# Eight chunks of x, six output stages and a new order list in a fused attention and S5 kernel

## The chip, the cores and the metric

The kernel runs on one core of a Trainium2 chip. The metric is device time in microseconds, the median of several runs. One further execution was taken with the hardware profiler; all rows below come from it.

## What is computed

Two layers over 2048 tokens of width 448, their outputs side by side (896 columns, bf16). Part A is sliding, dilated attention with 16 heads of 28: each token attends to itself and to the tokens 2, 4, ... 14 before it. Part B is a diagonal complex state-space layer (S5).

```python
# A: W, dil = 8, 2
qkv = (x @ wqkv).reshape(B, S, 3, H, Dh)           # q, k, v
idx = pos[:, None] - arange(W) * dil                # 8 keys per query, masked where idx < 0
o = softmax(q . k[idx] * Dh ** -0.5) . v[idx]
a = o.reshape(B, S, D) @ wo
# B: Lam = Lambda_re + i Lambda_im, Lam_bar = exp(dt * Lam)
Bu = x @ B_bar.T
for t in range(L):
    h = Lam_bar * h + Bu[:, t]
y = 2.0 * (h @ Cmat.T).real + x * Dskip
out = concatenate([a, y], -1)
```

## The kernel before

Since the window steps by two, even and odd tokens never meet in part A. The kernel views x as 1024 rows that hold an even and an odd token side by side (896 columns), and keeps it transposed in xA, columns on partitions in seven chunks of 128 (chunk 3 holds the last 64 columns of the even token and the first 64 of the odd one). An odd token so begins in the middle of a chunk, and the tile Wt of the weights holds a second copy for it, shifted by 64 partitions, in chunks 3 to 6; the steps s1v, s2v, s1k, s2k, s1q, s2q make it.

The program is a set of named steps, each with an engine and, where it writes to a double PSUM bank, the number of that bank (U0 to U3). ORDER, a list in the source, says in which order they are written out; so it fixes the order on each engine and on each DMA queue, and the framework adds the waits. A token such as w2f.P0 is the step w2f on TensorE (P) into bank 0; V is VectorE, A ScalarE, G GpSimd, S SyncE, which issues transfers. The steps named in the text:

- xt, xe: 128 rows of x are transposed on TensorE and copied to xA (rows 0 to 511); xa: the remaining rows are transposed by transfers on SyncE.
- v, k, q with a row block 0 to 7: the projections, two times six full matmuls (f, or e and o for the even and odd token) and two of 64 rows (t); ve, ke, qe copy the result out; kt and qt transpose k and q by a transfer.
- b, be, ri, sc, ro, with k and a half 0 or 1: the state-space input, its copy, the rotation, the scan and the rotation back into h. lam, c1, c2 mix the weights of part B (c1 and c2 read CT); g, ge and gp make Gm.
- s, x, a, n with a block and a parity: scores, exp, the products with v, and the normalisation into a tile O. ot transposes O into OT by a transfer on SyncE. Block 8 is the border between blocks; oc0, oc1, oc2 copy its columns from OTb into OT for the blocks 1 to 3, 4 and 5, 6 and 7, and so need ot8 and the ot of these blocks.
- wol loads the output weights wo, in four transfers, into the place of CT. w with a block: OT times wo, as f and t; y with a block: h times C and Gm times x, two parities; it starts from xd, which puts x times Dskip (from the tile xo, loaded by xol) into the odd bank. we and ye cast a bank into an output stage of the tile ys; wo0 to wo7 and yo send a stage to HBM on SyncE. The last y block is split into ya7, yb0, yb1.

A bank is written again when its last reader is done. The score tile s is a single one: a step s waits for the x before it. The list before, from the load of xo on:

```
xol.G a41.P1 ge1.A0 s51.P ri11.V g0.P0 x51.A n4.V1 s80.P ge0.A0 c26.V ot4.S a50.P1 sc110.V x80.A a51.P1 wol.S g2.P0 n5.V1 gp2.A0
s60.P ge2.V0 x60.A a80.P1 ot5.S xd1.V0 n8.V1 y1.P0 sc111.V ot8.S xd0.V1 ro11.V s61.P y0.P1 x61.A ri21.V ye1.A0 yo1.S oc0.A a60.P0
sc210.V ye0.A1 yo0.S a61.P0 s70.P n6.V0 w3t.P1 x70.A w3f.P1 sc211.V ot6.S w0f.P0 we3.A1 wo3.S ro21.V w0t.P0 oc1.A s71.P we0.A0 wo0.S
...
```

The tile ys has ten stages of [2, 448] and lies in the place of Wt; five buffers of rows serve the transposes of q and three those of k; two scratch tiles serve the weight mixes.

Of the kernel before, what the change touches and what calls it, by code (L numbers as in the profile page):

```python
# [37 lines left out]
s11.P tc23.G n0.V1 k5t.P0 x11.A k5f.P0 wtx2.S c24.V a10.P1 ri00.V tc21.G qt3.S ke5.A0 s20.P a11.P1 x20.A q7t.P0 xb1.S
q7f.P0 n1.V1 s21.P qe7.A0 c23.V k6f.P1 x21.A c21.V tc22.G k6t.P1 sc000.V a20.P0 qt4.S ke6.A1 s30.P sc001.V a21.P0
tc20.A kt6.S b20.P1 c22.V x30.A n2.V0 tc25.G kt4.S ro00.V kt5.S s31.P be20.A1 b11.P0 x31.A ot0.S c25.V ri20.V qt5.S  # L40
b31.P1 be11.A0 qt6.S c20.V sc200.V s40.P be31.A1 vg1.S b01.P0 tc12.A tc16.V qt7.S x40.A c16.V c12.V tc15.G ot1.S
sc201.V tc10.A s41.P be01.A0 c10.V a30.P1 a31.P1 c15.V tc14.A b21.P0 vg2.S n3.V1 x41.A tc11.G c14.V ot3.S kb.G c11.V
tc13.A s50.P ot2.S be21.A0 c13.V tc26.G a40.P1 ro20.V x50.A g1.P0 xol.G a41.P1 ge1.A0 s51.P ri11.V g0.P0 x51.A n4.V1
s80.P ge0.A0 c26.V ot4.S a50.P1 sc110.V x80.A a51.P1 wol.S g2.P0 n5.V1 gp2.A0 s60.P ge2.V0 x60.A a80.P1 ot5.S xd1.V0
n8.V1 y1.P0 sc111.V ot8.S xd0.V1 ro11.V s61.P y0.P1 x61.A ri21.V ye1.A0 yo1.S oc0.A a60.P0 sc210.V ye0.A1 yo0.S a61.P0
s70.P n6.V0 w3t.P1 x70.A w3f.P1 sc211.V ot6.S w0f.P0 we3.A1 wo3.S ro21.V w0t.P0 oc1.A s71.P we0.A0 wo0.S w4f.P1 x71.A
ri31.V w5f.P0 w5t.P0 w4t.P1 sc310.V w1t.P2 we4.A1 wo4.S w2t.P3 w1f.P2 we5.A0 wo5.S xd3.V1 w2f.P3 ro31.V we1.A2 wo1.S
# [106 lines left out]
def kernel(  # L154
# [80 lines left out]
    def xbar_x(dst, src, p, n):  # L235
        SP.dma_start_transpose(dst[:, :, n * p:n * p + n], src[n * p:n * p + n, :])
# [12 lines left out]
    SP.dma_start(Wt[0:64, 3, KQ], A_wqkv[384:448, KQ])  # L249

# [82 lines left out]
    def evac(e, o, i):  # L333
        if e == "A":
            ACT.copy(o, i)  # L335
        elif e == "G":
            G.tensor_copy(o, i)
        else:
            V.tensor_copy(o, i)  # L339
# [10 lines left out]

    def paired(name, ps, x, c, w):

        def sums(e, u_, js, tail):
            for j in js:
                seen = begun.setdefault((name, j), set())
                first = not seen
                seen.add(tail)
                if tail:
                    r = slice(64 * j, 64 * j + 64)
                    PE.matmul(ps(u_)[j], x()[r, 3, c], w()[r, 3], start=first, stop=not first, skip_group_check=True)  # L360
                for k in range(0 if tail else 3):
                    PE.matmul(ps(u_)[j], x()[:, 4 * j + k, c], w()[:, 4 * j + k], start=(k == 0 and first), stop=(k == 2 and not first), skip_group_check=True)  # L362
# [121 lines left out]

    for n, cols in (("v", VC), ("k", KC), ("q", QC)):
        def f(e, u_, cols=cols):
            evac(e, Wt[0:64, 4:7, cols], Wt[64:128, 0:3, cols])
# [4 lines left out]
        step["s2" + n] = f
    for b_, (n, i, lo, hi) in enumerate((("0a", 0, 0, 3), ("0b", 0, 3, 7), ("1", 1, 0, 7), ("2", 2, 0, 7), ("3", 3, 0, 7))):
        def xt(b_=b_, w=hi - lo):
            return held_by("x")[b_ % 3][:, 0, :].bitcast(BF16)[:, 0:128 * w].rearrange("p (k t) -> p k t", k=w)

        def f(e, u_, xt=xt, i=i, lo=lo, hi=hi):
            for k in range(lo, hi):
                PE.transpose(xt()[:, k - lo, :], xn[:, i, 128 * k:128 * k + 128], eye[:])
# [20 lines left out]
    def _(e, u_):  # L520
# [58 lines left out]
    for b in range(8):  # L579
        paired(f"v{b}", two, lambda: xA, slice(128 * b, 128 * b + 128), lambda: Wt[:, :, VC])  # L580
# [397 lines left out]
```

## Time and profile before

| | |
|---|---|
| median of 3 runs | 133.15 us |
| lowest, highest | 132.99, 133.58 us |
| the profiled execution's own time | 133.44 us |
| its span, first to last instruction | 131.6 us |
| busy: PE, PEld, DVE, ACT, POOL | 123.5, 63.2, 107.3, 86.6, 47.8 us |
| DMA | 20.83 MB, 158 GB/s on average |

PE is TensorE (PEld its weight loads, which overlap it), DVE VectorE, ACT ScalarE, POOL GpSimd, SP SyncE; SPq is SyncE's transfer queue. L362 is line 362 of the kernel. In a timeline a row gives start, length, engine, line, operation, tile written and tiles read, shape, and in brackets the idle time ahead of it with what ended it. A matmul's length includes its way through the array, so that consecutive ones overlap: what a group costs is read from the start of the next group.

### The profile page before, as it was taken

To read this page: it belongs to the slowest core of one execution; us is meant where nothing else is said; L and a number is where in the kernel's file an instruction comes from. 1 tells how busy PE (TensorE), PEld (TensorE's weight loads), DVE (VectorE), ACT (ScalarE), POOL (GpSimd) and SP (SyncE) were. 2 spreads that over 40 slices of the span, in tenths; PEclk is the share of its full clock that TensorE was granted. 3 is DMA by queue.
4 is the path that set the end of the run, shared out by engine and by line. 5 is a ranking of instruction groups with operands and counts; after the bars stand their busy time and mean duration, and the time that the engine had idled before them with its cause. 6 is when DMAs were issued, how large, how long until landed. Compare 5 with 4: busy or idle time off the path is not lost.

```text
span 131.6 us, 3129 instructions
## 1 busy us (share of the span) xinstructions
PE 123.5 (94%) x1221; PEld 63.2 (48%) x1226; DVE 107.3 (81%) x225; ACT 86.6 (66%) x91; POOL 47.8 (36%) x75
## 2 busy tenths in 40 slices
PE   7899999999999999999999998799999999999960
PEld 2554444443444466544454656545644654445540
DVE  2569999998898999999999999999999999860000
ACT  3249779887999879968698957608797523222230
POOL 7998911899700946660077840000000000000000
PEclk9999999999999999999999999999999999999998
DMA  4999969799899995898979949890452652422222
GB/s 106 371 318 211 230 118 183 124 271 165 174 103 186 216 158 86 175 188 200 199 142 156 221 97 256 198 189 9 140 144 70 229 124 70 139 70 72 70 82 70
DMA packets 54546, 20.83 MB, mean 158 GB/s; under 512 B 46782, under 2 KB 54160, under 8 KB 54528
## 3 DMA queue, kind: packets, MB, share of 16 engines
q1 hardware_dynamic: 53376, 18.70, 69.4%
q0 software_dynamic: 656, 1.50, 4.0%
q10 hardware_dynamic: 496, 0.40, 0.9%
q8 instruction: 11, 0.18, 0.6%
q14 instruction: 7, 0.06, 0.2%
HBM read 5.30 MB, written 3.86 MB: 70 GB/s over the span
## 4 chain that ended last, share of the span: by engine, by line
PE 57%; DVE 29%; issue 4%; DMA 3%; POOL 2%; ACT 1%; SPq 0%; DVEq 0%
PE U L362 14%; PE U L851 11%; PE early L362 8%; PE late L851 4%; DVE rs L755 4%; PE U L854 3%; PE U L727 3%; DVE O L692 3%; PE U L360 3%; DVE natW L540 3%; DMA Wt<-in_A_wqkv_dram 3%; DVE C L540 3%; POOL wtmp L534 2%; DVE ra L742 2%; DVE rb L743 2%
## 5 line engine op out<-in xcount | busy, mean ns | idle before, releaser
L671 ACT ACTIVATE P<-s 128x1920 bf16<-128x1920 f32 (+1 forms) x16 | 28.6, 1786 | 5.7 <-PE s L649 5.6
L727 PE MATMUL U<-xB,WT 128*128 128x512 bf16 x93 | 22.1, 379 | 0.3
L362 PE MATMUL U<-Wt,xA 128*128 128x448 bf16 x90 | 19.7, 353 | 1.0 <-DVE Wt L339 0.5
L362 PEld LDWEIGHTS <-xA 128*128 128x128 bf16 x144 | 12.9, 98 | 15.1 <-issue 4.2
L534 POOL TENSOR_SCALAR wtmp<-CT,p_pah 128x448 f32<-128x448 bf16 x6 | 13.7, 2279 | 12.4 <-DVE rv L745 6.8
L335 ACT CAST ys<-U 128x896 bf16<-128x896 f32 (+1 forms) x11 | 9.5, 871 | 12.0 <-PE U L851 9.2
L851 PEld LDWEIGHTS <-h 128*128 128x128 bf16 x105 | 10.0, 98 | 9.2 <-DVE U L841 0.2
L727 PEld LDWEIGHTS <-WT 128*128 128x128 bf16 x98 | 9.2, 97 | 10.6
L362 PE MATMUL early<-Wt,xA 128*128 128x448 bf16 x54 | 11.7, 354 | 0.0
L335 ACT CAST u<-U 128x1024 bf16<-128x1024 f32 (+1 forms) x8 | 7.2, 905 | 4.5 <-PE U L727 4.4
L692 DVE TENSOR_TENSOR O<-U,rcs 128x896 bf16<-128x896 f32 (+1 forms) x9 | 9.8, 1090 | 0.3
L851 PE MATMUL U<-natW,h 128*128 128x448 bf16 x42 | 9.0, 353 | 0.1
L755 DVE TENSOR_TENSOR_SCAN rs<-p_r,ini,rv 128x512 bf16<-128x512 f32 x7 | 8.8, 1274 | 0.0
L680 PE MATMUL U<-Vt,P 128*128 128x29 bf16 x256 | 8.2, 176 | 0.6 <-DVE O L692 0.6
L755 DVE TENSOR_TENSOR_SCAN rs<-p_r,rv 128x512 bf16<-128x512 f32 x7 | 8.6, 1257 | 0.0
L680 PEld LDWEIGHTS <-P 128*128 128x128 bf16 x256 | 7.6, 96 | 2.1 <-issue 0.8
L335 ACT CAST ys<-late 128x896 bf16<-128x896 f32 (+2 forms) x6 | 4.3, 718 | 6.1 <-PE late L851 5.6
L362 PE MATMUL U<-wo,OT 128*128 128x448 bf16 x36 | 7.6, 353 | 0.0
L851 PE MATMUL U<-C,h 128*128 128x448 bf16 x35 | 7.4, 352 | 0.0
L335 ACT CAST Nx<-U 128x896 bf16<-128x896 f32 x7 | 6.4, 908 | 1.5 <-PE U L360 1.4
L534 POOL TENSOR_SCALAR wtmp<-CT,p_pag 128x448 f32<-128x448 bf16 x2 | 4.2, 2080 | 8.4 <-DVE C L540 8.4
L362 PEld LDWEIGHTS <-OT 128*128 128x128 bf16 x48 | 4.4, 98 | 4.9 <-issue 1.2
(198 smaller groups left out, 231.4 us busy)
## 6 DMA issues: line engine op xcount, KB each, us to landing
out_dram<-ys SPq DMA_DIRECT2D x15, 224.0 KB, 2.4
tmpB<-in_A_x_dram SPq DMA_DIRECT2D x4, 224.0 KB, 3.4
xo<-in_B_x_dram POOLq DMA_DIRECT2D x1, 896.0 KB, 8.0
Wt<-in_A_wqkv_dram SPq DMA_DIRECT2D x1, 672.0 KB, 5.8
wo<-in_A_wo_dram SPq DMA_DIRECT2D x2, 336.0 KB, 4.8
natW<-in_B_B_re_dram SPq DMA_DIRECT2D x1, 336.0 KB, 5.9
natW<-in_B_B_im_dram SPq DMA_DIRECT2D x1, 336.0 KB, 7.4
Wt<-in_A_wqkv_dram ACTq DMA_DIRECT2D x1, 224.0 KB, 3.5
```

The lines of the kernel that those rows point to most:

```text
L335: ACT.copy(o, i)
L360: PE.matmul(ps(u_)[j], x()[r, 3, c], w()[r, 3], start=first, stop=not first, skip_group_check=True)
L362: PE.matmul(ps(u_)[j], x()[:, 4 * j + k, c], w()[:, 4 * j + k], start=(k == 0 and first), stop=(k == 2 and not first), skip_group_check=True)
L534: (G if e == "G" else V).tensor_scalar(view(held_t[name][:]), src(), scale(), None, ALU.mult)
L540: V.scalar_tensor_tensor(view(dst()), src(), scale(), view(t[:]), ALU.mult, ALU.add)
L671: ACT.activation(pv[:, :, :, c0:128], s4[:, :, 0:4 * n].rearrange("p g (s q) -> p g s q", s=4), ACTF.Exp, scale=SCALE)
L680: PE.matmul(U[u_][:, q, 29 * hd:29 * hd + 29], P[:, hd // 4, hd % 4, :], Vt[:, b, q, hd, :], start=(hd == 0), stop=(hd == H - 1), skip_gro ...
L692: V.tensor_tensor(O[0:n, :].rearrange("p (t h d) -> p t h d", t=2, h=H), av[0:n, :, :, 0:DH], rc.unsqueeze(3).to_broadcast((n, 2, H, DH)), ...
L727: PE.matmul(U[u_][:, j, :], WT[:, i, 128 * m:128 * m + 128], xB[:, i, HALF * hf:HALF * hf + HALF], start=(i == 0), stop=(i == 6))
L755: V.tensor_tensor_scan(rs[0][:, i], p["r2"][:, k:k + 1].to_broadcast((128, HALF)), rv[0][:, i], 0.0 if hf == 0 else ini[:, m:m + 1], ALU.m ...
L851: PE.matmul(ps[:, 0:D], hb[:, m, lo:lo + 128], C1()[:, m, :] if par else natW[:, m, 0:D], start=(m == 0 and par == 0), stop=(m == 6 and pa ...
L854: PE.matmul(ps[:, 0:D], xB[:, k, tk], Gm[:, k, :], start=False, stop=(k == 3), skip_group_check=True)
```

## The change

x is laid out in eight chunks that begin at the columns 0, 128, 256, 384, 448, 576, 704 and 768. The odd token begins chunk 4, its last 64 columns are the upper half of chunk 7, and both tokens use the same weight chunks 0 to 2; the last 64 weight rows lie in both halves of chunk 3, put there by one transfer that reads them twice. The six weight copies go. Each block of 128 rows gets eight transposes in place of seven. xa2 becomes three transfers, xa3 two. Wt is smaller, so ys has six stages; q has seven row buffers and the weight mixes three scratch tiles. The list is new.

```diff
-spin spin spin spin spin spin sps sps sps xt0a.P xt0b.P xe0a.A co0.G s1v.V xe0b.A sps sps v0e.P0 nw.S s2v.V nt.G sps
-sps sps xt1.P v0o.P0 xe1.V xt2.P xt3.P xe2.A v1o.P1 xe3.V v0t.P0 v1t.P1 ve0.A0 v3t.P2 tr.P3 v1e.P1 s1k.V s2q.A s2k.V
...
+spin spin spin spin spin spin sps sps sps xt0a.P co0.G xt0b.P xe0a.A sps v0e.P0 xe0b.A spin xt1.P xt2.P nt.A xt3.P
+v0t.P0 xa2.S xe1.V xe3.V v0o.P0 xe2.A v3f.P1 ve0.A0 tr.P2 v3t.P1 k2t.P3 p1.V2 ve3.A1 p2.A q0t.P0 q0f.P0 k2f.P3 qe0.A0
+wr2.S p3.V q1f.P2 ta2.V ta3.V nw.S q1t.P2 ke2.A3 dia.G ta0.G v4t.P1 qe1.V2 ta1.A p4.A p5.A v5t.P0 xa3.S td1.V k0t.P3
...
+be11.A0 x40.A c26.V ri11.V a30.P0 a31.P0 s41.P tc15.A c10.V ot2.S c15.V tc13.G c13.V be21.A1 tc14.A x41.A b01.P1 s50.P
+tc12.G c14.V n3.V0 c12.V tc11.A tc16.G ot3.S be01.A1 a40.P0 a41.P0 vg2.G kb.G tc22.G x50.A xol.S c11.V c16.V n4.V0
+ro20.V g2.P1 s51.P gp2.A1 tc20.A g0.P0 x51.A ge2.V1 s80.P a50.P1 a51.P1 ge0.A0 g1.P0 x80.A c22.V ge1.A0 s60.P x60.A
+sc110.V n5.V1 c20.V a80.P1 xd1.V0 n8.V1 sc111.V xd0.V1 y1.P0 s61.P x61.A ye1.A0 yo1.S ot4.S ot8.S ro11.V ot5.S oc1.A
+ri31.V xd3.V0 y0.P1 ye0.A1 yo0.S s70.P x70.A y3.P0 sc310.V oc0.A ye3.A0 yo3.S a60.P1 ro31.V a61.P1 ri21.V n6.V1 s71.P
+wol.S x71.A w2t.P0 w2f.P0 sc210.V we2.A0 wo2.S w1f.P1 xd2.V2 sc211.V a70.P3 a71.P3 y2.P2 ot6.S w0f.P0 w0t.P0 ye2.A2
+yo2.S w1t.P1 n7.V3 we0.A0 wo0.S we1.A1 wo1.S ro21.V ot7.S oc2.A w3t.P3 w5t.P2 w3f.P3 w5f.P2 w6f.P0 w7t.P1 w6t.P0
+we3.A3 wo3.S ri01.V w4t.P3 we5.A2 wo5.S w4f.P3 sc010.V sc011.V ro01.V we6.A0 wo6.S we4.A3 wo4.S w7f.P1 xd6.V2 xd4.V0
+gu1.V xd5.V3 we7.A1 wo7.S y6.P2 ye6.V2 yo6.S gu2.P1 y5.P3 ye5.A3 yo5.S y4.P0 xdb.V2 ya7.P3 ye4.A0 yo4.S gu3.V1 flag.V
+ye7.A3 yp7.A xda.V1 yb0.P1 yf0.V1 yb1.P2 yf1.V2 yq7.S
...
-    xA = t_([128, 7, NP], BF16, "xA", "rA")
+    xA = t_([128, 8, NP], BF16, "xA", "rA")
-    Wt = t_([128, 7, 3 * D], BF16, "Wt", "rW")
+    Wt = t_([128, 4, 3 * D], BF16, "Wt", "rW")
...
+    CHUNK = (0, 128, 256, 384, D, D + 128, D + 256, D + 320)
...
+    def both_halves(cols):
+        src = A_wqkv[384:448, cols]
+        return Wt[:, 3, cols], bass.AP(src.tensor, src.offset, [[0, 2]] + [list(d) for d in src.ap])
-    ACT.dma_start(Wt[0:64, 3, VC], A_wqkv[384:448, VC])
+    ACT.dma_start(*both_halves(VC))
-    SP.dma_start(Wt[0:64, 3, KQ], A_wqkv[384:448, KQ])
+    SP.dma_start(*both_halves(KQ))
...
-                    PE.matmul(ps(u_)[j], x()[r, 3, c], w()[r, 3], start=first, stop=not first, skip_group_check=True)
+                    PE.matmul(ps(u_)[j], x()[r, tail2 if j else 3, c], w()[r, 3], start=first, stop=not first, skip_group_check=True)
-                    PE.matmul(ps(u_)[j], x()[:, 4 * j + k, c], w()[:, 4 * j + k], start=(k == 0 and first), stop=(k == 2 and not first), skip_group_check=True)
+                    PE.matmul(ps(u_)[j], x()[:, 4 * j + k, c], w()[:, odd * j + k], start=(k == 0 and first), stop=(k == 2 and not first), skip_group_check=True)
...
-        step[f"xa{n}"] = lambda e, u_, n=n: xbar_x(xA, xA2, n, 256)
+            SP.dma_start_transpose(xA[:, 0:4, tk], xA2[tk, 0:512])
+            SP.dma_start_transpose(xA[:, 4:7, tk], xA2[tk, D:D + 384])
+            if n == 2:
+                SP.dma_start_transpose(xA[:, 7, 512:NP], xA2[512:NP, 2 * D - 128:2 * D])
...
-    free_y = list(range(10))
+    free_y = list(range(6))
```

For v, k and q the new arguments are odd=0 and tail2=7; for w they are as before.

More of the change, by code (lines that the diff above doesn't have):

```diff
@@ L38 @@
[L38 to L47, printed above, removed]
@@ L498, in f @@
             for k in range(lo, hi):
-                PE.transpose(xt()[:, k - lo, :], xn[:, i, 128 * k:128 * k + 128], eye[:])
+                c = CHUNK[k]
+                PE.transpose(xt()[:, k - lo, :], xn[:, i, c:c + 128], eye[:])
         step[f"xt{n}"] = f
@@ L524, in _ @@
         Q[e].dma_start(Pt[64:128, :], B_B_re[384:448, :])
-    tmps = [t_([128, D], F32, f"wtmp{i}") for i in range(2)]
+    tmps = [t_([128, D], F32, f"wtmp{i}") for i in range(3)]
     held_t = {}
@@ L567, with f @@
     step["xb0"] = lambda e, u_: xbar_x(xB, xB2, 0, 512)
-    for n in range(1, 4):
-        step[f"xa{n}"] = lambda e, u_, n=n: xbar_x(xA, xA2, n, 256)
+    for n in range(2, 4):
+        def f(e, u_, n=n):
+            tk = slice(256 * n, 256 * n + 256)
+            SP.dma_start_transpose(xA[:, 0:4, tk], xA2[tk, 0:512])
+            SP.dma_start_transpose(xA[:, 4:7, tk], xA2[tk, D:D + 384])
+            if n == 2:
+                SP.dma_start_transpose(xA[:, 7, 512:NP], xA2[512:NP, 2 * D - 128:2 * D])
+        step[f"xa{n}"] = f
     step["xb1"] = lambda e, u_: xbar_x(xB, xB2, 1, 512)
@@ L579 @@
     for b in range(8):
-        paired(f"v{b}", two, lambda: xA, slice(128 * b, 128 * b + 128), lambda: Wt[:, :, VC])
+        paired(f"v{b}", two, lambda: xA, slice(128 * b, 128 * b + 128), lambda: Wt[:, :, VC], 0, 7)
         def f(e, u_, b=b):
```

40 lines of the change are left out of this document (16 added, 24 removed).

## Prediction

> **What bounds the kernel now.** I read the page first, then busy time by stretches, then the chain of waits in order of time, and last the SyncE queue's own timeline. From the page and the stretches (columns: length; busy us and instructions of PE, PEld, DVE, ACT, POOL; granted clock; DMA share; GB/s):
>
> ```profile
> PE 123.5 (94%) x1221; PEld 63.2 (48%) x1226; DVE 107.3 (81%) x225; ACT 86.6 (66%) x91; POOL 47.8 (36%) x75
> ...
> 33.00:60.00 27.00, 26.53 (x350) 13.60 (x351) 25.75 (x42) 23.50 (x20) 13.82 (x14) 1.00 0.95 161
> 60.00:84.80 24.80, 23.06 (x344) 13.02 (x345) 23.90 (x40) 20.06 (x19) 9.17 (x6) 1.00 0.89 178
> 84.80:127.00 42.20, 42.20 (x338) 21.98 (x339) 31.45 (x54) 18.82 (x22) 0.00 (x0) 1.00 0.42 116
> 127.00:131.60 4.60, 0.29 (x6) 0.12 (x3) 0.00 (x0) 0.59 (x2) 0.00 (x0) 0.86 0.18 58
> ```
>
> TensorE has something in hand for 94% of the span. Between 33 and 84.8 us it stands idle only 0.47 + 1.74 = 2.2 us, and after 84.8 not at all; VectorE is nearly as full up to 84.8. Then the chain of waits (start, length, what):
>
> ```profile
> 84.08 0.65 DVE U L841
> ...
> 84.77 1.50 PE U L851 x7
> ...
> 125.95 0.97 PE late L894 x7
> ...
> 126.94 0.66 ACT ys L335 x2
> ```
>
> Step y1, the first of the y outputs, starts at 84.77 right behind a VectorE step (xd1). From there to 126.92 the chain is TensorE alone. So two things can change the time: when y1 starts, and whether TensorE still runs without a gap afterwards.
>
> **The change part by part.** What goes away first:
>
> ```profile
> 4.84 1.88 DVE L339 COPY Wt<-Wt 64x1344 bf16<-64x1344 bf16 x2 [3.09 <-DMA Wt<-in_A_wqkv_dram]
> 9.05 1.37 DVE L339 COPY Wt<-Wt 64x1344 bf16<-64x1344 bf16 x2
> 11.52 0.67 DVE L339 COPY Wt<-Wt 64x1344 bf16<-64x1344 bf16 x1
> ```
>
> ```profile
> 6.78 0.73 PE L362 MATMUL U<-Wt,xA 128*128 128x448 bf16 x3 [0.47 <-DVE Wt L339]
> 7.34 0.94 PE L499 MATMUL x<-eye,tmpB 128*128 128x128 bf16 x14
> ```
>
> Five weight copies leave VectorE, 1.88 + 1.37 + 0.67 = 3.92 us (the sixth was ScalarE's), and the first odd-row sums no longer wait 0.47 us for one. Four transposes are added, 0.94 / 14 = 0.067 us each, 0.27 in all; the matmuls of v, k, q stay as many as they were. VectorE is late at y1, so its relief brings y1 forward. By how much isn't shown: at most the 3.92 removed, at least the 2.2 in which TensorE stood idle, if the new list lets both go; or nothing, if y1 meets something else. I take the middle of 2.2 and 3.92, 3.05, because TensorE's own work ahead of y1 is nearly unchanged and it has little more to give up. y1 moves by -3.05 - 0.47 + 0.27 = -3.25 us, to 81.5.
>
> Now the new list behind y1. Read by engine, it says: SyncE yo1, ot4, ot8, ot5, yo0, yo3, wol, wo2, ot6, yo2, wo0, wo1, ot7; ScalarE x61, ye1, oc1, ye0, x70, oc0, ye3, x71, we2, ye2, we0, we1, oc2, we3; TensorE y1, s61, y0, s70, y3, a60, a61, s71, w2t, w2f, w1f, a70, a71, y2, w0f, w0t, w1t, w3t, w5t, w3f, w5f, w6f. In the old list wol stood behind ot4, and ot5 and ot8 too stood ahead of yo1. SyncE's queue, in the old run:
>
> ```profile
> 72.06 9.55 SPq L698 DMA_TRANSPOSE OT<-O  x3
> 81.71 0.54 SPq L825 DMA_DIRECT2D wo<-in_A_wo_dram  x1
> ...
> 84.21 1.24 SPq L698 DMA_TRANSPOSE OT<-O  x1
> 86.81 1.21 SPq L701 DMA_TRANSPOSE OTb<-O  x1
> 91.58 2.34 SPq L882 DMA_DIRECT2D out_dram<-ys  x2
> ```
>
> ```profile
> 80.28 0.67 DVE L540 SCALAR_TENSOR_TENSOR natW<-CT,p_sah,wtmp 128x448 bf16<-128x448 bf16 x1
> ```
>
> Three transposes of O take 9.55 us of the queue though one takes 1.24: the last of them, ot4, waits for its normalisation, and wol, free to go when the last mix has read CT (80.28 + 0.67 = 80.95), starts only at 81.71 behind it. A transfer whose input is late therefore holds all that stand behind it. In the new list wol stands behind yo3, which waits for ye3, and ye3 for y3; ot4, ot8 and ot5 stand behind yo1, which waits for ye1. The lengths of the steps, TensorE then ScalarE:
>
> ```profile
> 88.28 0.38 PE L645 MATMUL s<-msk 32*128 32x480 bf16 x4
> ...
> 88.81 1.50 PE L851 MATMUL U<-natW,h 128*128 128x448 bf16 x7
> ...
> 92.22 0.96 PE L680 MATMUL U<-Vt,P 128*128 128x29 bf16 x32
> 93.11 0.38 PE L645 MATMUL s<-msk 32*128 32x480 bf16 x4
> ...
> 110.43 1.30 PE L362 MATMUL U<-wo,OT 128*128 128x448 bf16 x6
> ...
> 113.29 1.49 PE L851 MATMUL late<-natW,h 128*128 128x448 bf16 x7
> ```
>
> ```profile
> 88.98 1.77 ACT L671 ACTIVATE P<-s 128x1920 bf16<-128x1920 f32 x1 [4.33 <-PE s L649]
> 90.65 0.90 ACT L335 CAST ys<-U 128x896 bf16<-128x896 f32 x1
> 91.44 0.34 ACT L335 COPY OT<-OTb 128x168 bf16<-128x168 bf16 x1
> ...
> 108.69 0.28 ACT L335 COPY OT<-OTb 128x112 bf16<-128x112 bf16 x1 [0.56 <-DMA OT<-O]
> ```
>
> An s step takes 88.81 - 88.28 = 0.53 us, a y step 92.22 - 88.81 = 3.41, a pair of a steps 93.11 - 92.22 = 0.89, two w units 113.29 - 110.43 = 2.86 (one 1.43: six full matmuls, f, 1.14, a pair of half ones, t, 0.28). On ScalarE x starts 0.70 after its s and holds the engine 90.65 - 88.98 = 1.67; an output cast takes 0.90, a border copy (oc) 0.3. The last of these rows shows ScalarE idle for 0.56 us until OT had landed: oc holds the engine, and all behind it. Transfers (KB each, us from issue to landing):
>
> ```profile
> out_dram<-ys SPq DMA_DIRECT2D x15, 224.0 KB, 2.4
> ...
> xo<-in_B_x_dram POOLq DMA_DIRECT2D x1, 896.0 KB, 8.0
> ...
> wo<-in_A_wo_dram SPq DMA_DIRECT2D x2, 336.0 KB, 4.8
> ...
> OT<-O SPq DMA_TRANSPOSE x8, 3.2
> ```
>
> Four wo issues take 84.21 - 81.71 = 2.5 us, 0.6 each; an O transpose takes 1.3 with its gap.
>
> Put together, in us from the end of y1: s61 to 0.5; x61 0.7 to 2.4; ye1 to 3.3; yo1 is issued at 3.3, ot4 at 3.9, ot8 at 5.2, ot5 at 6.5, which lands 3.2 later, at 9.7. Until then oc1 holds ScalarE, and behind it ye0, though y0 was done at 3.9. oc1 to 10.0, ye0 to 10.9, x70 to 12.4, oc0, ye3 to 13.6. TensorE meanwhile: y0 to 3.9, s70 to 4.5, y3 to 7.9; a60 needs the bank that ye0 frees: it stands until 10.9; a61 to 11.8; s71, when x70 is read, to 13.0. SyncE: yo3 at 13.6, wol's four transfers at 14.2, 14.8, 15.4 and 16.0, and the last lands 4.7 later, at 20.7. w2f, which needs it, starts at 20.7. Without a wait it would start at 0.53 + 3.41 + 0.53 + 3.41 + 0.89 + 0.53 + 0.28 = 9.6. First term: 20.7 - 9.6 = 11.1 us, nothing hides it, for TensorE's order has nothing else in that place. Its bounds: if wo lands as fast as an output of 224 KB, 2.4 us, it is 8.8; as slowly as its own 4.8 in the old run, 11.2. I take wo's own figure, the same transfer.
>
> Second term, from w2f's start: we2 done at 2.0, ot6 issued behind wo2 at 2.7; yo2 waits for ye2, which waits for y2 (1.14 + 1.14 + 0.89 + 3.41 = 6.6), so 7.5; wo0 waits for we0 (8.9), wo1 for we1 (9.8); ot7 goes at 10.4, lands at 13.6, and oc2 is done at 13.9. w6f needs that copy, and TensorE is there at 6.6 + 1.14 + 0.28 + 0.28 + 0.56 + 2.28 = 11.1. It stands 2.8 us; with outputs issued a little earlier, 2.0, with transposes a little slower, 3.5.
>
> VectorE is held too: n6 waits for a61, n7 for a71, and with them the rest of the second half's chain:
>
> ```profile
> 104.22 0.36 DVE L691 RECIPROCAL rcs<-U 128x32 f32<-128x32 f32 x1
> ...
> 112.31 0.42 DVE L767 TENSOR_TENSOR h<-ra,rb 128x512 bf16<-128x512 bf16 x1
> ```
>
> From n7's start to the end of ro01 it took 112.73 - 104.22 = 8.5 us; a71 is done 3.2 after w2f's start, so ro01 could be at 11.7, and y6, which needs it, comes seven w pieces behind oc2, at 18.2: covered, with 6.5 us to spare for ro21, which stands between them now.
>
> Third term, the clock. TensorE stands from 13.0 to about 20. Its first six matmuls after standing, and the group of the same shape later:
>
> ```profile
> 0.85 2.72 PE L508 MATMUL x<-const-bfloat16-1.0 128*128 128x512 bf16 x6 [0.85 <-PEq L962]
> ```
>
> ```profile
> L727 PE MATMUL U<-xB,WT 128*128 128x512 bf16 x93 | 22.1, 379 | 0.3
> ```
>
> Six take 2.72 us, 0.45 each, against 22.1 / 93 = 0.24: a start from rest loses 2.72 - 6 x 0.24 = 1.3 us. In the last stretch above the granted clock is 0.86, with TensorE at rest for 4.3 of 4.6 us, so it falls within such a rest. I add 1.3; bounds 0 and 2.6 (if the earlier rest of 3 us counts too).
>
> The Trainium skill, page "TensorE: Matmul & The Clock Gate", section "What's actually happening", has the clock halved after an idle window of about 3.4 us until about 3.4 us of work have passed. By it the loss would be 1.7, an estimate, and the sum 0.4 higher; the cadence of the first six agrees with a halved clock.
>
> The Trainium skill, page "DMA: Bandwidth & Descriptors", section "Anatomy of one DMA — SWDGE (gpsimd) path", fits a transfer as 2.0 us plus its bytes at 436 GB/s. By that an estimate for 336 KB is 2.8 us where the trace has 4.8; the sum would be 1.9 lower.
>
> Edits with one answer: six output stages instead of ten cost nothing, since a stage is asked for again six outputs later and lands 2.4 us after issue; more row buffers and queries' buffers only loosen; the last casts move from ScalarE to VectorE, both free there. The larger transfers at the start and the third scratch are priced under the rivals.
>
> Sum against the profiled execution: 131.6 - 3.25 + 11.1 + 2.8 + 1.3 = 143.55 us of span. The execution's own time was 133.44, 1.84 more than its span, and it stands 0.29 above the median of 133.15. 143.55 + 1.84 - 0.29 = **145.1 us**. With all terms at their low ends (y1 earlier by 4.1, 8.8, 2.0, 0) 139.9; at the high ends (y1 unmoved, 11.2, 3.5, 2.6) 150.5.
>
> **The rivals.** A: ScalarE isn't held at oc1, because ot5 has landed by the time ye0 can run (3.9). Then ye0 is done at 4.8, ye3 at 9.2 (y3, x70 and oc0 ahead of it), wo goes from 9.9 and lands at 16.4, and the first term is 6.8: 140.8 us. For it: two of the three oc copies waited for nothing before. Against: ot5 stands behind yo1, ot4 and ot8.
>
> B, the faster one: SyncE's queue doesn't hold what stands behind a waiting transfer, so that wo and the O blocks land in time. All three terms fall away: 131.6 - 3.25 + 1.55 = 129.9. It decides where wol goes out by 9.6 - 4.7 - 1.8 = 3.1 after y1. For it: VectorE's relief and TensorE's idle time ahead of y1 are real. Against: the stretch of 9.55 us above, and oc copies that ScalarE runs in order.
>
> C: the front comes late. In the old run two x transposes kept the queue for a long time:
>
> ```profile
> 7.47 6.59 SPq L236 DMA_TRANSPOSE xA<-in_A_x_dram  x2
> ```
>
> ```profile
> 3.71 0.69 PE L499 MATMUL x<-eye,tmpB 128*128 128x128 bf16 x7
> ```
>
> 3.3 us for fourteen blocks each. The first now has eighteen, 4.2 us, and v4 asks for it behind 32 transposes (2.1 us) and five units of v, k and q (about a w unit each, 7.2 in all) that begin at 3.71: with 1 us of waits, at 14. Issued at 7.47 at the latest and landed 4.2 to 8.0 later, it is in time or 1.5 us late, and the weights' doubled last rows, 168 KB more ahead of it, could add 1: 147.6.
>
> D, the change doesn't do what it says: y1 isn't earlier, since xd1 meets xo, whose landing took 8.0 us and whose issue now stands behind ot3 on SyncE. Then 148.4.
>
> **How the numbers follow.** Forecast 0.69, A 0.10, B 0.07, C 0.07, D 0.05, and 0.02 for terms that cancel. A measurement of this kernel tells about 0.5% from no change. All but B and the cancelling case are slower by more: slower 0.91, same 0.02, faster 0.07. The range reaches from A with a faster landing of wo, 138.5, to D, 149.0; what it leaves out is B, the lowest ends of A and the highest of the forecast.
>
> **What would show it.** In the new profile: no copies into Wt on VectorE; y1's group near 81.5; ScalarE idle some 6 us ahead of a border copy, released by a transfer into OT; TensorE idle 3 us before an a step (released by a cast), then 6 to 8 us before a w group, released by wo, with the granted clock below 1 in that slice; a second wait of 2 to 3 us before w6. If wo's four issues begin before y3 ends, or if TensorE has no gap behind y1, the prediction is wrong at its main step; if the gaps are there and y1 isn't early, only at the first.

## The result, and the profile after

The changed kernel takes 160.08 us (159.69 to 160.24) against 133.31 in the same rounds: 1.2005 times as long [1.1967, 1.2044]. The profiled execution took 159.69, its span is 158.0. Some executions of a version run slower as a whole: the ratios and their intervals leave them out, the medians hold them, and the profile of e11 below is of one. The page (busy us and share; granted clock in 40 equal slices):

```profile
PE 129.7 (82%) x1227; PEld 65.5 (41%) x1227; DVE 104.0 (66%) x222; ACT 86.3 (55%) x91; POOL 42.5 (27%) x69
...
PEclk9987659999999999999999999999755999999999
```

TensorE, idle for 131.6 - 123.5 = 8.1 us before, now has 158.0 - 129.7 = 28.3 us of idle time. Its own timeline shows where: what it waits for is in the brackets.

```profile
7.95 1.36 PE L499 MATMUL x<-eye,tmpB 128*128 128x128 bf16 x16 [1.36 <-DMA tmpB<-in_A_x_dram]
10.32 0.41 PE L367 MATMUL U<-Wt,xA 64*128 64x448 bf16 x2 [1.02 <-DMA Wt<-in_A_wqkv_dram]
10.67 3.47 PE L369 MATMUL U<-Wt,xA 128*128 128x448 bf16 x9
20.73 0.18 PE L386 MATMUL early<-eye,rows 28*64 28x28 bf16 x1 [6.59 <-ACT xA L341]
...
96.28 1.48 PE L857 MATMUL U<-natW,h 128*128 128x448 bf16 x7
...
111.11 0.96 PE L686 MATMUL U<-Vt,P 128*128 128x29 bf16 x32 [3.16 <-ACT ys L341]
112.78 0.51 PE L651 MATMUL s<-msk 32*128 32x480 bf16 x4 [0.71 <-ACT P L677]
...
118.07 0.53 PE L367 MATMUL U<-wo,OT 64*128 64x448 bf16 x1 [4.38 <-DMA wo<-in_A_wo_dram]
119.24 0.53 PE L367 MATMUL U<-wo,OT 64*128 64x448 bf16 x1 [0.64 <-DMA wo<-in_A_wo_dram]
119.70 4.13 PE L369 MATMUL U<-wo,OT 128*128 128x448 bf16 x12
123.67 0.96 PE L686 MATMUL late<-Vt,P 128*128 128x29 bf16 x32
...
134.98 1.31 PE L369 MATMUL U<-wo,OT 128*128 128x448 bf16 x6 [2.56 <-ACT OT L341]
```

From y1 on it is the forecast's picture: a60 stands 3.16 for ye0's bank, w2t, and with it w2f, 4.38 and 0.64 for wo, w6f 2.56 for the border copy. From y1's start to the end the old span had 131.6 - 84.77 = 46.83 us, the new one 158.0 - 96.28 = 61.72: 14.9 more, where the three terms sum to 15.2. Ahead of y1 it is another picture: y1 starts at 96.28, not 81.5. The step tr, at 9.46 before, starts at 20.73. TensorE's row of it before:

```profile
9.46 0.20 PE L379 MATMUL early<-eye,rows 28*64 28x28 bf16 x1
```

The stretches from the start to tr and from tr to y1, of after and then of before (length; busy us of PE, PEld, DVE, ACT, POOL; clock; DMA share; GB/s):

```profile
0.00:20.73 20.73, 10.14 (x59) 4.80 (x59) 2.30 (x17) 3.43 (x5) 4.69 (x12) 0.84 0.98 174
20.73:96.28 75.55, 74.10 (x830) 37.86 (x830) 69.19 (x149) 63.81 (x66) 37.86 (x57) 0.98 0.86 158
```

```profile
0.00:9.46 9.46, 7.84 (x59) 4.16 (x59) 4.28 (x18) 3.42 (x5) 8.45 (x22) 1.00 0.84 262
9.46:84.77 75.31, 73.10 (x827) 36.90 (x830) 71.53 (x154) 63.80 (x64) 39.38 (x54) 1.00 0.96 175
```

The whole loss of the front, 11.3 us, is ahead of tr; from tr to y1 nothing was gained. ScalarE's queue, and then ScalarE, in that time:

```profile
15.27 0.52 ACTq L521 DMA_DIRECT2D natW<-in_B_B_re_dram  x1
16.31 0.47 ACTq L522 DMA_DIRECT2D natW<-in_B_B_im_dram  x1
18.50 0.47 ACTq L523 DMA_DIRECT2D Gm<-in_B_B_im_dram  x1
19.01 0.61 ACTq L524 DMA_DIRECT2D Gm<-in_B_B_re_dram  x1
19.66 1.01 ACT L341 COPY xA<-x 128x1024 bf16<-128x1024 bf16 x1 [14.53 <-DMA WT<-in_B_B_im_dram]
...
109.97 0.28 ACT L341 COPY OT<-OTb 128x112 bf16<-128x112 bf16 x1 [6.92 <-DMA OT<-O]
110.16 0.90 ACT L341 CAST ys<-U 128x896 bf16<-128x896 f32 x1
```

The new list issues nt, four small loads that nobody needs soon, on ScalarE (nt.A; GpSimd had them, nt.G). They go out only at 15.27 to 19.01, and the copy xe2 and all else on ScalarE stand behind them. Why they are so late, the program's own list of waits says (a lane is one of eight counters, DMAHW0 to 7, that the framework gives to the transfers of SyncE and ScalarE in turn; GpSimd's have others):

```
SP   L254 DMA Wt<-in_A_wqkv_dram 128x3x896
SP   L255 DMA Wt<-in_A_wqkv_dram 128x1x896 [waits DMAHW0_49]
SP   L571 DMA_TRANSPOSE xA<-in_A_x_dram 128x4x256 [waits DMAHW1_49]
ACT  L521 DMA natW<-in_B_B_re_dram 64x448 [waits DMAHW7_49]
ACT  L522 DMA natW<-in_B_B_im_dram 64x448 [waits DMAHW1_49]
ACT  L523 DMA Gm<-in_B_B_im_dram 64x448 [waits DMAHW3_49]
ACT  L524 DMA Gm<-in_B_B_re_dram 64x448 [waits DMAHW4_49]
```

A transfer waits until the one that had its lane before has landed. nt's first waits for lane 7, the load of the weights of k and q (L254); the others for transposes of x and of B, which are later still. The trace bears this out: the transfers waited for land at 15.25, 16.29, 18.48 and 18.96, and each of the four is issued within 0.06 us of it. The load of L254 is slow, 12.0 us to landing (the issues view: KB, us to landing). Beside it a stretch of 1 us, with the columns of the stretches above:

```profile
Wt<-in_A_wqkv_dram SPq DMA_DIRECT2D x1, 672.0 KB, 12.0
```

```profile
11.00:12.00 1.00, 1.00 (x4) 0.44 (x3) 0.00 (x0) 0.00 (x0) 0.00 (x0) 0.50 0.13 50
```

This is one of four microseconds, 10 to 14, that look alike in DMA: 50 to 52 GB/s at a share of 0.13, what two busy engines of sixteen would make. What runs there is the doubled read of the last 64 weight rows, and the load of L254 lands only when it is over; with plain transfers in its place (e1) that load lands 6.6 us after its issue. The Trainium skill, page "DMA: Bandwidth & Descriptors", section "Why a DMA increments its semaphore by 16 and not by 1", says that a transfer is carried by the largest number of engines, up to 16, that divides the slowest dimension of both access patterns. The change's source pattern begins with a dimension of 2. By that rule two engines carry it, and the trace agrees: 0.13 is 2/16. So does the counter of v's doubled read: it moves at the issue (2.56) and then only twice, at 9.81 and 10.28, where that of the first plain load of weights moves sixteen times.

### The profile page after: what moved, and what is told of

It reads as the page before. It is cut to its first block, busy times and chain, and to the rows that moved or that the text cites. A ratio compares the mean times of both kernels' runs of the same rounds, so it can differ in the third digit from the quotient of the medians.

```text
span 158.0 us, 3134 instructions
## 1 busy us (share of the span) xinstructions
PE 129.7 (82%) x1227; PEld 65.5 (41%) x1227; DVE 104.0 (66%) x222; ACT 86.3 (55%) x91; POOL 42.5 (27%) x69
## 4 chain that ended last, share of the span: by engine, by line
PE 44%; DVE 16%; DMA 16%; SPq 10%; ACT 7%; issue 3%; ACTq 1%; DVEq 0%
PE U L369 13%; PE U L733 9%; PE early L369 5%; DMA xB<-in_B_x_dram 5%; PE late L857 4%; SPq L571 4%; DMA OT<-O 4%; ACT P L677 3%; DVE rs L761 3%; PE U L367 3%; DMA xA<-in_A_x_dram 2%; DVE O L698 2%; DMA wo<-in_A_wo_dram 2%; DMA Wt<-in_A_wqkv_dram 2%; SPq L572 2%
## 5 line engine op out<-in xcount | busy, mean ns | idle before, releaser
L369 PE MATMUL U<-Wt,xA 128*128 128x448 bf16 x102 | 24.4, 384 | 0.2 <-ACT xA L341 0.2
L733 PE MATMUL U<-xB,WT 128*128 128x512 bf16 x91 | 20.8, 380 | 0.6 <-DMA xB<-in_B_x_dram 0.6
L341 ACT CAST ys<-U 128x896 bf16<-128x896 f32 x9 | 8.0, 906 | 10.1 <-PE U L369 6.8
L341 ACT CAST ys<-late 128x896 bf16<-128x896 f32 (+1 forms) x6 | 5.0, 842 | 12.9 <-PE late L857 11.2
L534 POOL TENSOR_SCALAR wtmp<-CT,p_pag 128x448 f32<-128x448 bf16 x4 | 6.0, 1493 | 20.5 <-DVE natW L540 18.0
L341 ACT COPY xA<-x 128x384 bf16<-128x384 bf16 (+2 forms) x3 | 2.1, 730 | 14.8 <-DMA WT<-in_B_B_im_dram 14.5
L686 PE MATMUL U<-Vt,P 128*128 128x29 bf16 x224 | 6.9, 176 | 3.2 <-ACT ys L341 3.2
L369 PE MATMUL early<-Wt,xA 128*128 128x448 bf16 x42 | 8.9, 353 | 0.0
L259 POOL TENSOR_SCALAR_AFFINE_SELECT Gm<-Gm 32x128 bf16<-32x128 bf16 (+2 forms) x16 | 7.1, 452 | 1.0 <-issue 0.2
L651 PE MATMUL s<-msk 32*128 32x480 bf16 (+1 forms) x64 | 6.3, 380 | 1.2 <-ACT P L677 1.2
```

Of the source, the lines that this page charges most:

```text
L259: G.affine_select(o, i, pat, op, fill, base=base, channel_multiplier=ch)
L369: PE.matmul(ps(u_)[j], x()[:, 4 * j + k, c], w()[:, odd * j + k], start=(k == 0 and first), stop=(k == 2 and not first), skip_group_check= ...
L534: (G if e == "G" else V).tensor_scalar(view(held_t[name][:]), src(), scale(), None, ALU.mult)
L651: PE.matmul(s4[:, g, 0:4 * n].rearrange("p (s q) -> p s q", s=4), msk[32 * g:32 * g + 32, 0, :], msk[32 * g:32 * g + 32, 1:2, c0:c0 + n].t ...
L686: PE.matmul(U[u_][:, q, 29 * hd:29 * hd + 29], P[:, hd // 4, hd % 4, :], Vt[:, b, q, hd, :], start=(hd == 0), stop=(hd == H - 1), skip_gro ...
L733: PE.matmul(U[u_][:, j, :], WT[:, i, 128 * m:128 * m + 128], xB[:, i, HALF * hf:HALF * hf + HALF], start=(i == 0), stop=(i == 6))
```

## The experiments

All ratios are to the kernel before, run in the same rounds. **One repair at a time, of the changed kernel.** e1: the last rows by plain transfers.

```diff
-    ACT.dma_start(*both_halves(VC))
-    SP.dma_start(*both_halves(KQ))
+    for r in (0, 64):
+        ACT.dma_start(Wt[r:r + 64, 3, VC], A_wqkv[384:448, VC])
...
+        SP.dma_start(Wt[r:r + 64, 3, KQ], A_wqkv[384:448, KQ])
```

> The changed kernel with one edit: the last 64 weight rows are put into the two halves of chunk 3 by two plain transfers each, in place of one that reads them twice. Theory 1 (the doubled transfers themselves are slow and hold the queue: the weights of q and k landed 12.0 us after issue, where they took 5.8 before): the weights land within 6 to 7 us, the first x transposes keep SyncE's queue 3 to 4 us instead of 6.7, y1 starts 8 to 11 us earlier than 96.3, total 149 to 152 us. Theory 2 (the four transfers of nt, now issued by ScalarE, hold that engine until transfers ahead of them have landed): ScalarE still stands there until about 14 to 16 us, y1 gains 0 to 5 us, total 155 to 160.

Measured: 155.24 us, 1.165 [1.161, 1.170]; 4.8 less. TensorE's timeline has one long wait left, and ScalarE's shows that nt still holds it:

```profile
16.05 0.18 PE L388 MATMUL early<-eye,rows 28*64 28x28 bf16 x1 [6.13 <-ACT xA L343]
```

```profile
14.98 1.01 ACT L343 COPY xA<-x 128x1024 bf16<-128x1024 bf16 x1 [9.52 <-DMA natW<-in_B_B_im_dram]
```

e2: `nt.A` becomes `nt.G` in the list.

> The changed kernel with nt issued by GpSimd again, in the same place of the list. Theory 2 (ScalarE held by nt): the step tr comes at about 9.5 to 14 us instead of 20.7 and y1 6 to 11 us earlier, total 149 to 154. Theory 1 (slow doubled transfers): tr comes at 14, but the first k sums wait for their last weight rows until 16 or later; y1 gains 3 to 5 us, total 155 to 157.

Measured: 154.95 us, 1.162 [1.158, 1.167]; 5.1 less. ScalarE is free, and now the doubled read itself is met (first the chain of waits, then TensorE's timeline):

```profile
4.15 11.79 DMA Wt<-in_A_wqkv_dram
```

```profile
15.98 0.36 PE L367 MATMUL early<-Wt,xA 64*128 64x448 bf16 x2 [2.95 <-DMA Wt<-in_A_wqkv_dram]
```

e3: in the list, ot4 behind n4, ot5 behind n5, wol behind c20, ot8 behind n8, ot6 behind n6, n7 behind a71, ot7 behind n7.

> The changed kernel with SyncE's order mended behind y1 alone: ot4, ot5 and ot8 right behind their normalisations, wol ahead of yo1, ot6 and ot7 right behind theirs. The prediction's mechanism (SyncE's order holds oc1, wo and oc2): the waits of 3.2, 0.7, 4.4, 0.6 and 2.6 us on TensorE go, and with them the slow clock behind them; y1 unmoved at 96, total 143 to 147. Rival (VectorE's chain of the second half is as late and takes the place of these waits): y6 waits for ro01, total 150 or more.

Measured: 145.21 us, 1.088 [1.081, 1.094]; 14.9 less, and TensorE has no wait left behind y1. e4: e1, e2 and e3 together.

> All three edits together. If front and back add: y1 at 84 to 87, no wait behind it, total 131 to 135. If the front's loss is mostly something else (the early, larger transposes of x), y1 stays at 88 or later and the total above 136.

Measured: 135.51 us (134.71 to 136.44), 1.020 [1.015, 1.024]; 24.6 less, where the single repairs sum to 24.8; y1 is back from 96.28 to 85.18. Its TensorE, with what is left at the start, y1, w2f and what follows w2f:

```profile
11.44 0.35 PE L369 MATMUL early<-Wt,xA 64*128 64x448 bf16 x1 [1.23 <-DMA Wt<-in_A_wqkv_dram]
...
85.18 1.49 PE L859 MATMUL U<-natW,h 128*128 128x448 bf16 x7
...
98.41 2.70 PE L371 MATMUL U<-wo,OT 128*128 128x448 bf16 x12
100.94 0.96 PE L688 MATMUL late<-Vt,P 128*128 128x29 bf16 x32
```

**The forecast's terms one by one,** each put back into e4. e9: ot6, n7 and ot7 where the change has them.

> The version with the three repairs (135.5 us), with ot6, n7 and ot7 back at their places in the changed list, that is ot7 behind yo2, wo0 and wo1: the forecast's second term by itself. By its working TensorE stands 2.8 us (2.0 to 3.5) ahead of w6f, for the copy that waits for ot7: 137.5 to 139.0 us. Rival: the second term is only there because the wait for wo had shifted the work ahead of it; then 135.5 within 0.5 and no wait ahead of w6f.

e10: wol behind yo3, and ot6 behind it.

> The version with the three repairs (135.5 us), with the load of wo behind yo3 and ot6 behind it; ot4, ot5 and ot8 stay early, so that ScalarE isn't held. The forecast's rival A by itself: wo goes from 9.9 after y1's end and lands at 16.4, w2f stands 6.8 us, so 142.3 us, up to 143.6 with the slow clock after so long a rest. Rival theory (wo late alone makes the whole of the first term): 11 us, 146.5.

e11: ot4, ot8, ot5 behind yo1, as in the change; wol stays early.

> The version with the three repairs (135.5 us), with ot4, ot8 and ot5 back behind yo1 and wo early: the hold of ScalarE by itself. By the forecast's working the copy that waits for ot5 is done 10.0 us after y1's end and a60 starts at 10.9 instead of 7.9: 3.0 us, so 138.5 us, up to 139.8 with the clock. Rival theory (the bank of ye0 isn't what a60 waits for, or the copy isn't held): 135.5 within 0.5.

TensorE's waits behind y1 in e9, then e10, then e11:

```profile
114.11 1.31 PE L371 MATMUL U<-wo,OT 128*128 128x448 bf16 x6 [2.50 <-ACT OT L343]
```

```profile
102.96 0.35 PE L369 MATMUL U<-wo,OT 64*128 64x448 bf16 x1 [3.78 <-DMA wo<-in_A_wo_dram]
104.13 0.53 PE L369 MATMUL U<-wo,OT 64*128 64x448 bf16 x1 [0.82 <-DMA wo<-in_A_wo_dram]
104.59 4.66 PE L371 MATMUL U<-wo,OT 128*128 128x448 bf16 x12
109.05 1.06 PE L688 MATMUL late<-Vt,P 128*128 128x29 bf16 x32
```

```profile
87.63 1.49 PE L859 MATMUL U<-natW,h 128*128 128x448 bf16 x7
...
102.50 1.01 PE L688 MATMUL U<-Vt,P 128*128 128x29 bf16 x32 [3.20 <-ACT ys L343]
104.17 0.59 PE L653 MATMUL s<-msk 32*128 32x480 bf16 x4 [0.66 <-ACT P L679]
...
105.69 3.81 PE L371 MATMUL U<-wo,OT 128*128 128x448 bf16 x12
```

e9 took 139.25 us, 1.050 [1.044, 1.057], just above the 137.5 to 139.0 expected. Of its profiled execution's 139.00 - 134.71 = 4.3 us over e4's, the wait ahead of w6f is 2.50; the rest is that y1 came 1.9 later (87.10), with a longer wait for part B's x ahead of it (1.23 at 62.39, in e4 0.22).

e10 took 140.99 and 142.86 us (143.15 is the median of all four, and there is no ratio), against 142.3 to 143.6 expected. In its profile, of the execution of 142.86, y2 starts 109.95 - 86.19 = 23.8 us behind y1, in e4 101.76 - 85.18 = 16.6, so 7.2 later. The 12 matmuls behind the wait take 109.05 - 104.59 = 4.46 us, where e4's take 2.53: 1.9 of the 7.2 is the clock (0.50 from 103.4 to 110.2), and 5.2 the wait, against 6.8 expected.

e11 took 140.99, 1.057 [1.053, 1.061], 5.5 above e4, more than the 3.0 to 4.3 expected: the expectation counted a60's 3.0 and left out what the forecast has behind it, s71 that waits for x70 (by the forecast's own working s71 is done at 13.0 instead of 9.3, so w2f 3.7 late; it is 105.69 - 87.63 = 18.1 behind y1's start where e4's is 13.2, so 4.8 late, and the group of 12 behind it is 3.81 long, in e4 2.70). The rivals that saw no wait in e9 and e11, and the whole first term in e10, fall.

**The layout apart from the list.** e5: the changed kernel with the old list less its six copy steps, and e1's transfers.

> The changed layout, with the list of the kernel before less its six copy steps, six output stages, and the last 64 weight rows brought by two plain transfers per part. Theory 1 (the forecast's first step: VectorE is late at y1 and its relief of 3.9 us brings y1 forward): y1 near 81.5 instead of 84.8, no new wait behind it, so 130.0 us. Theory 2 (TensorE has 80.3 us of work in the 84 us ahead of y1 in both lists, so that VectorE's relief can't shorten it): y1 at 84.3 to 85.3, 132.8 to 133.8 us. Theory 3 (eighteen blocks of x in the transposes of rows 512 to 1023 instead of fourteen come late, whatever the list): TensorE waits 1 to 2 us for xA, 134.5 to 135.5 us.

Measured: 135.94 us, 1.020 [1.015, 1.025]; none of the three theories. xa2 is in time; TensorE waits once for long, for part B's x, and SyncE's queue shows when that was issued, here and then in the kernel before:

```profile
34.85 1.67 PE L735 MATMUL U<-xB,WT 128*128 128x512 bf16 x6 [2.08 <-DMA xB<-in_B_x_dram]
```

```profile
24.87 5.38 SPq L236 DMA_TRANSPOSE xB<-in_B_x_dram  x1
```

```profile
23.49 4.44 SPq L236 DMA_TRANSPOSE xB<-in_B_x_dram  x1
```

The five transposes of x ahead of it take 1.60 + 2.50 + 1.26 + 1.99 + 1.29 = 8.64 us of SyncE's queue, the old two 6.59; so it goes 1.4 later. It also keeps the queue 0.9 longer, and why is not shown. e6: the same with the doubled read.

> As the run before, but with the doubled read of the last 64 weight rows that the change has. Theory of the doubled read (carried at about 51 GB/s, it lands about 12 us after its issue for k and q and 7 for v, whatever the list): v0t, which stood at 8.8 in the old list, waits 1 to 1.5 us for the part of v, and k1t, which stood at 12.5, waits 3 to 3.5 us for that of k and q, so 4 to 5 us above the run before. Rival (the doubled read costs only what it costs ScalarE's queue, which the old list doesn't use for it): the same as the run before within 0.7 us.

Measured: 139.04 us, 1.043 [1.038, 1.048]; 3.1 above e5, where 4 to 5 were expected. TensorE waits 0.62 for v's part and 1.92 for that of k and q, less than expected; rows of x come late ahead of it (0.64, 0.33 and 0.34). And it isn't the doubled read alone that is late. From the waits of SyncE's queue (total, times, longest):

```profile
SPq L517 <- DMA Wt<-in_A_wqkv_dram: 3.1, 1, 3.1
```

L517 is the second transfer of nw, into natW. It needs nothing of Wt; its lane, 2, is that of v's doubled rows, and it stands 3.1 us until they have landed, with the transposes of x behind it. e7: e4 with the four plain transfers on GpSimd; e8: e5 with them there.

> The new list with all three repairs, and the four plain transfers of the last weight rows issued by GpSimd, so that the load of the weights of k and q is the seventh transfer of SyncE and ScalarE together instead of the ninth. If transfers of SyncE and ScalarE wait for the one eight before them: that load goes out at 3.2 to 3.3 instead of 4.2, k2t no longer waits 1.6 us, and the time is 134.0 to 134.8 us against 135.5 of the version without it. If the wait for that load is a matter of bandwidth: 135.5 within 0.5.

> The layout in the old list, with the four plain transfers of the last weight rows issued by GpSimd. If TensorE's work sets the time ahead of y1: 132.6 to 133.6 us, at most 0.4 below the same with the transfers on SyncE and ScalarE. If VectorE's relief counts: 130 us. Against it: GpSimd's issues come ahead of the vectors that tr needs, so tr could be late and p1 with it, 0.5 to 1 us more.

Measured: e7 134.23 us, 1.006 [1.003, 1.009], as expected by the lanes and against bandwidth: the big load goes at 3.15, and no wait for Wt is left. But rows of x and the vectors for tr then come 0.5 to 0.65 us late, so that y1 starts at 85.4. e8 135.29, 1.011 [1.007, 1.014], above both figures expected: xb0 in time, tr 2 us late, for rows of x and for its vectors. b3: e5 with `xb0.S` moved behind `wr0.S`.

> The layout in the old list with plain tail transfers (135.9 us), with the transpose of the first 512 rows of part B's x (xb0) moved on SyncE ahead of the transposes of the mixed weights and of q. Theory 1 (the layout's additional transposes push SyncE's queue back by 1.4 us and more, xb0 lands 2.1 us after TensorE asks for it, and nothing else is wrong): y1 near 84.8, 133.5 to 134.2 us. Theory 2 (VectorE's relief is there but hidden behind this wait): y1 at 82 to 83, 131 to 132 us. Rival (the queue is short of time as a whole and something else comes late in its place): 135 to 136 us.

Measured: 137.04 us, 1.030 [1.027, 1.033]: xb0 in time, and instead waits of 0.58 for WT, 0.44 and 1.12 for Kt. Something else comes late in its place, the rival, though at 1 us more than its 135 to 136. b2: the layout in the old list with the old five row buffers and two scratch tiles; nw, and of the plain transfers one per part, on GpSimd.

> The layout alone in the old list, with the old number of row buffers and scratch tiles; nw and one of the two plain transfers per part go to GpSimd, which takes 1.7 us of issues off SyncE's queue ahead of xb0. Theory (all that the layout costs in the old list is SyncE's queue, 2 us for five transposes of x in place of two): xb0 lands in time, y1 at 84.3 to 85, 133.0 to 133.9 us. Rival (SyncE is late elsewhere as well, as when xb0 alone was moved): 135 to 136 us. If VectorE's relief is worth its 3.9 us once the queue is in time: 130 to 131 us.

Measured: median 134.12 us, 1.0014 [0.998, 1.005], so no difference. TensorE's timeline in b2:

```profile
80.38 0.96 PE L688 MATMUL U<-Vt,P 128*128 128x29 bf16 x32 [0.62 <-DVE O L700]
83.54 1.06 PE L690 MATMUL U<-Vb,P 105*56 105x29 bf16 x32 [0.80 <-DVE O L700]
84.73 1.50 PE L859 MATMUL U<-natW,h 128*128 128x448 bf16 x7
```

and in the kernel before:

```profile
80.41 0.96 PE L680 MATMUL U<-Vt,P 128*128 128x29 bf16 x32 [0.62 <-DVE O L692]
83.57 1.06 PE L682 MATMUL U<-Vb,P 105*56 105x29 bf16 x32 [0.80 <-DVE O L692]
```

Without the copies, y1 starts 0.04 us earlier, behind the same two waits for VectorE. The wait of 0.47 for a copy is gone too, and the four transposes added use up most of it: tr starts at 9.31 in place of 9.46. b4: b2 with the six copies back at their places, into a tile that nobody reads.

> As the version b2, with the six weight copies of the old kernel put back at their old places, into a tile that nobody reads: VectorE's (and ScalarE's) work of the old kernel without its use. Theory (TensorE has 80 us of work in the 84 ahead of y1, and VectorE is not late before 12 us, where the copies lie): the same as b2 within 0.6 us. Rival (the forecast's first step, VectorE's relief counts): 2.2 to 3.9 us slower than b2.

Measured: median 135.05 us, 1.013 [1.010, 1.016], 1.2% above b2: neither. The two waits near y1 are again 0.63 and 0.80, so the copies don't reach VectorE's late stretch. What this version loses lies early: by 54.66, where b2 is at 53.20, TensorE is as late as at y1. VectorE ahead of the step p1, and TensorE behind it:

```profile
12.14 0.62 DVE L347 COPY spare<-Wt 64x1792 bf16<-64x1792 bf16 x1 [1.48 <-ACT spare L343]
```

```profile
13.63 0.37 PE L369 MATMUL early<-Wt,xA 64*128 64x448 bf16 x2 [0.49 <-DVE dsr L398]
```

The tile that nobody reads is one for all six copies, where the old kernel's went to different columns of Wt: VectorE stands 1.48 us until ScalarE's copy has written it, p1 comes behind that, and TensorE 0.49 behind p1. The old kernel has no such wait. So b4 shows that the copies don't act at y1, but it doesn't price them: its 1.2% holds a wait that they never had.

**The two waits, and the new list's start.** b5: b2 with `ri11.V` behind n4 and `sc110.V` behind n8; b6: the kernel before with the same two moves. b1: e4 with v1's units ahead of k2, k2f ahead of k2t, nw and half of the plain transfers on GpSimd.

> The layout in the old list (version b2), with two VectorE steps taken out of the way ahead of y1: ri11 goes behind n4, and sc110 behind n8. Theory (what TensorE waits for ahead of y1 is not the amount of VectorE's work but the order of its last steps: 0.62 us until n4 has read the bank, 0.80 us until n5 has): both waits go, y1 starts at 83.3 to 83.6 instead of 84.7, and VectorE, which has 11 us to spare behind y1, catches up: 131.6 to 132.0 us. Rival (what is put off comes late behind y1): 133.0 to 133.5 us.

> The kernel before, with the same two steps moved and nothing else. Theory (VectorE's order ahead of y1 decides, and the weight copies at the start of the program have no part in it): the same gain as with the layout, 131.6 to 132.0 us, within 0.4 of that version. Rival (the relief at the start counts once the order no longer hides it): the version with the layout is faster by 0.8 us and more.

> The new list with the repairs (135.5 us), and three further ones at the start: the units of v1, which the changed list has in the middle, go between v3t and k2, with k2f ahead of k2t; of the four plain transfers of the last weight rows one of each part goes to GpSimd; the two transfers nw go to GpSimd too. Theory (what is left of the loss at the start is that k2 is asked for 1.6 us before its weights land): no wait for Wt, y1 near 83.6 instead of 85.2, 133.8 us or, with the scatter of the version before taken off too, 133. Rival (SyncE's queue or VectorE then comes late in the middle): y1 stays at 85, 135 to 135.5 us.

Measured: b5 135.31 us (median), 1.009 [1.006, 1.012], b6 133.62, 1.0018 [1.0004, 1.0032]; 131.6 to 132.0 was expected of both. In b6 the two waits shrink to 0 and 0.19, y1 starts at 83.84, and the next thing is late (TensorE, then VectorE):

```profile
83.84 1.50 PE L852 MATMUL U<-natW,h 128*128 128x448 bf16 x7 [0.36 <-DVE U L842]
88.80 1.48 PE L852 MATMUL U<-natW,h 128*128 128x448 bf16 x7 [0.86 <-DVE U L842]
```

```profile
83.15 0.63 DVE L842 TENSOR_TENSOR U<-xo 128x448 f32<-128x448 bf16 x1 [0.26 <-DMA xo<-in_B_Dskip_dram]
```

The 0.93 us won ahead of y1 is spent by y0, which waits for VectorE's xd0; in b5 xd1 meets xo as well and stands 1.20. So the order of VectorE's late steps does set y1, as the theory has it, but the gain is not kept; and the layout is no faster here either, against the rival. b1 took 134.28, 1.009 [1.006, 1.012], between the two times expected: the waits for Wt are gone, and y1 stays at 85.4, as the rival has it, with short waits in the middle in their place (0.21 for WT, 0.27 for xB, 0.27 and 0.38 for ScalarE, 0.35 for VectorE). No version beat the kernel before.

## Why the prediction was wrong

The direction and the mechanism behind y1 were right. The first step was wrong, by 96.28 - 81.5 = 14.8 us, which is nearly all that the time is off (160.08 against 145.1).

- **First step, y1 3.25 us earlier (failed).** It came 11.5 later. Two things were wrong in it. The gain was taken between TensorE's 2.2 us of idle time and VectorE's 3.92 us of copies, as if the copies were the cause of the idle time. The copies lie ahead of 12.2 us; the waits for VectorE that could have gone, 0.62 and 0.80, lie at 80 and 83 us; and what was saved at one place did not reach the other: b2 shows 0.04 us, where the step adds up to 3.25. And the cost at the start, left to rival C at 2.5 us, was of another kind: the doubled read on two engines (e1: 4.8) and ScalarE held by nt (e2: 5.1); in e4, without both, y1 starts at 85.18. The `nt.A` stood in the quoted list and was not weighed, though the forecast itself argued that a waiting transfer holds what is behind it; what it waits for, lanes, no row of the old profile shows.
- **First term, 11.1.** w2f starts 119.70 - 96.28 = 23.4 us behind y1's start, in e4 13.2: 10.2 (TensorE's idle time in it is 3.16 + 0.71 + 4.38 + 0.64 = 8.9; the rest goes in the matmuls right behind the waits). wo's last transfer is issued at 116.29, 20.0 behind y1's start (16.0 behind its end of 3.4 forecast, 19.4); TensorE's last wait for wo ends at 119.24, some 3 us on, where 4.7 was taken. The late issue and the quick landing partly cancel.
- **Second term, 2.8:** 2.56, and 2.50 by itself (e9).
- **Clock, 1.3:** the 12 matmuls behind the wait take 123.67 - 119.70 = 3.97 us against 2.53, so 1.4; a60 and s71 behind the rest of 3 us lose little. What was left out is the clock in the front, 0.50 while nine matmuls took 3.47.
- **The sum of the three**, 15.2, lies closer to the 14.9 measured than its terms do, and that is chance: the terms measure 10.2 + 2.56 + 1.4 = 14.2, and 0.7 comes from elsewhere, since e4, which has none of the three, also needs 132.7 - 85.18 = 47.5 us from y1 on against 46.8.
- **Rival A** did not happen (oc1 held ScalarE 6.92 us); its price, 6.8, came out in e10 as 5.2 of waiting and 1.9 of slow clock. **Rival C** named the right place, the front, with a wrong mechanism and a wrong price. **D**'s meeting with xo was seen only in b5 and b6, where y1 comes earlier.
- Six stages in place of ten cost nothing, as said: no step waits for a stage.

What stays open: what the copies alone were worth at the start, since b2 changes other things with them and b4 adds a wait; and what makes up the last 2% of e4. In its profiled execution, the fastest of four, 0.4 us of that lies ahead of y1 and 0.7 behind it; b1 takes the waits for Wt away and gains 1% at most.

## What to carry to other kernels

Time saved on an engine counts only at the place where another engine waits for it: read the row whose wait should vanish, and see that the work removed stands directly ahead of it. A run that puts the work back must not add a wait of its own. For every transfer that a change adds or moves, ask which queue it stands in, what it waits for besides its data, and what stands behind it. One leading dimension of 2 in an access pattern can cost more than the work it saves.

## What the hardware showed unexpectedly

- While a read of 112 KB done twice by a leading dimension of 2 is under way, DMA moves 50 GB/s at a share of 0.13. It lands after 11.8 us (e2); as two plain transfers it lands after 6.6 (e1) to 6.8 (e4).
- In this program transfers of SyncE and ScalarE share eight completion lanes: the ninth waits for an earlier one to land, whichever engine issued it. The wait is in the issuing engine's order and holds its computing too (ScalarE for 14.53 us). The lanes are the framework's doing, and no line of the kernel shows them.
- The granted clock falls to 0.50 behind rests shorter than 3.4 us. In the change it falls at 112.9 us, behind the rest of 3.16 and ahead of that of 4.38; in the 3.4 us before, TensorE was busy for 1.08. It falls at 10.5 too, behind waits of 1.36 and 1.02, and there TensorE was busy for 1.41 of the 3.4 us before. The Trainium skill, page "TensorE: Matmul & The Clock Gate", section "What's actually happening", has a halved clock after an idle window of about 3.4 us. In e10 the trace agrees: a rest of 3.78 ends at 102.96, and the clock falls at 103.4. In the change it doesn't, if the window has to be idle throughout: TensorE worked for about a third of it.
